# Top-k attention and a mixture of experts on one core: the first head pair in two halves of 128 tokens, and four places for fetched first parts

## Chip, cores, metric

One NeuronCore of a Trainium2 chip runs the whole program. The metric is the device time of one execution in microseconds (us). Engines: TensorE (PE; its weight loads PEld), VectorE (DVE), ScalarE (ACT), GpSimd (POOL) and SyncE (SP), which issues nearly all DMA transfers.

## What is computed

Four batches of eight heads with 576 tokens and head size 64: scores, the 32 largest of each row kept, softmax over them, times the values. The result, 2304 tokens of 512, goes through eight experts (512 to 1024, relu, back to 512), weighted per token by a gate that is normalised eight times over rows and columns.

```python
scores = scale * np.matmul(q, k.transpose(0, 1, 3, 2))
kth = np.partition(scores, -top_k, axis=-1)[..., -top_k:-top_k + 1]
scores = np.where(scores >= kth, scores, -1000000000.0)
attn = np.exp(scores - np.max(scores, axis=-1, keepdims=True))
attn = attn / (np.sum(attn, axis=-1, keepdims=True) + 1e-09)
x = np.matmul(attn, v)                # per head, then (2304, 512)
for e in range(E):
    h = np.maximum(x @ w1[e], 0.0)
    out += P[:, e:e + 1] * (h @ w2[e])   # P: normalised gate
```

## The kernel before, in words

**Attention.** Heads are taken in pairs (`attend_heads`), tokens in blocks of 256. Per head pair and block, `weight_tiles` takes two tiles of 128 tokens (t = 0, 1). For each tile and each of the two heads TensorE makes the scores (L122, L123), ScalarE copies them out of PSUM (`s`, L134), and VectorE finds the 32 largest in four rounds of the eight largest (L144) with three replacements between (L147), seven top-k operations per unit. ScalarE then weighs (L150, L151), GpSimd scales (L203), TensorE transposes (L274) and ScalarE stores the transposed weights in `at` (L291). After both tiles `weigh_values` multiplies with the values (L281), and ScalarE copies the result into the token tile `xt` (L304). `board` splits it into a high and a low part (`xh` on ScalarE by L83, `xl` on VectorE by L89).

**Experts.** `xh` and `xl` hold two seats of 256 tokens each: columns 0 to 255 and 256 to 511. A block sits in a seat for eight turns (`visit`), one expert per turn. Block 0 boards at turn 0, block 1 at turn 4, so in turns 0 to 3 (experts 0 to 3, `ALONE`) block 0 is alone and the second seat's columns stand idle. In those lone turns and the four after them (`LATER`, experts 4 to 7), part of the first layer of block 0 is made earlier, in plain fp32 from `xt`: `first_quarter` (L524, head pair 0 only, experts 4 to 7) and `first_half` (L537, head pairs 0 and 1, experts 0 to 3). Each result is copied out of PSUM (`y`, L512) and written to DRAM (L514). `second_half` fetches it again into one buffer `yp` (L546), multiplies the rest of the head pairs (L488) and adds the fetched part on VectorE (L552). `store_hidden` writes the hidden values (`hh` L556, `hl` L557), and L601 is the second layer.

**Order.** The program is written with priorities: attention high, the first parts low. A scheduler places the instructions of each engine in a fixed order; on the chip each engine, and SP's queue, works through its own order and waits at the head for what is not ready. Weights come into three buffers `wr`; `split_weights` converts them (`wh` on ScalarE L83, `wl` on GpSimd L86). Six such conversions for lone turn 0 are issued inside `first_half`. The places that the first parts take:

```python
for s in range(4):                                   # first_quarter, per expert
    ps = ps1.tile([128, 2, 256], F32, name="p1")     # ps1: two PSUM buffers
    for fo in range(2):
        nc.tensor.matmul(ps[:, fo, :], wr[:, s, fo * 128:(fo + 1) * 128], x[:, 0, :], start=True, stop=True)
    part(e, s, ps)                                   # ScalarE copy, then a write of 256 KB
```

Of the kernel before, what the change touches and what calls it, by code (L numbers as in the profile page):

```python
# [7 lines left out]
F32 = mybir.dt.float32  # L8
F32R = mybir.dt.float32r
U16 = mybir.dt.uint16  # L10
AF = mybir.ActivationFunctionType
# [4 lines left out]
DM, E, F = 512, 8, 1024  # L16
# [30 lines left out]
ALONE, LATER = range(0, 4), range(4, 8)  # L47
WR, WB, XR, NS, RAW, YB = 3, 6, 3, 3, 3, 4
# [3 lines left out]
def kernel(  # L52
# [11 lines left out]
    nc = tc.nc  # L64
    BIG = 1000000
# [181 lines left out]
        if not phases:  # L247
            attend_rest(hp, load_q("qm", 1024, 256, 1), ks, vr, xm)

    def weight_tiles(qs, ks, put, on_pool=False, crossed=None, plain=None):  # L250
        for t in range(2):
            Et = ap_.tile([128, 2, S], F32, name="Et", bufs=2)
            st = ap_.tile([128, 2, 2], F32, name="st", bufs=3)
            units = []
            for i in range(2):
                o = i * 256 + t * 128
                qc = qs[:, o:o + 128]
                if plain is not None and t == 0:
                    sp = plain_scores(plain[0][va if i == 0 else vb, o:o + 128], plain[1 + i][va if i == 0 else vb, :])
                else:  # L260
                    sp = scores([((a, 0, 288), [(qc, ks[i], slice(a * 288, a * 288 + 288))]) for a in range(2)])
                units.append((copy_scores(sp[:, :, 0:288]), Et[:, i, :], st[:, 0, i:i + 1]))
            topk(units, crossed is not None)
            normalise(Et, st, 2, on_pool)
            cs = slice(t * 128, (t + 1) * 128)
            if crossed is not None:
                cross(Et, crossed[:, :, cs])
                continue
            Ef = Et.rearrange("p a b -> p (a b)")
            for g in range(3):  # L270
                ps = pst.tile([128, 4, 128], F32, name="pt")
                for r in range(3):
                    j = g * 3 + r
                    nc.tensor.transpose(ps[:, r, :], Ef[:, j * 128:j * 128 + 128], idt)  # L274
                put(slice(g * 3, g * 3 + 3), cs, ps[:, 0:3, :])

    def weigh_values(av, vr, at, n, order):
        for j in order:
            for i, r in enumerate((va, vb)):
                o, block = (256 * i + 64 * j, 5 * i + j) if j < 4 else (512 + 64 * i, 4)  # L280
                weighed = nc.tensor.matmul(av[r, 0:n], vr[:, o:o + 64], at[:, block, 0:n], start=(j == order[0]), stop=(j == order[-1]))  # L281
        with tc.issue_after(weighed.ins):
            while ungated:
                gate_logits(*ungated.pop(0))

    def attend_phase(b, hp, qs, qm, ks, vr, xt, xm, plain=None):
        nq = 256 if xm is None else 320
        at = ap_.tile([128, 9, 320], F32, name="at", bufs=1)

        def put(blocks, cs, src):  # L290
            nc.scalar.activation(at[:, blocks, cs], src, AF.Copy)  # L291

        crossed = at if len(X) > 4 else None
        weight_tiles(qs, ks, put, b == 0 or crossed is not None, crossed, plain)
        if xm is not None:
            def put_rest(rows, blocks, src):
                nc.scalar.activation(at[rows, blocks, 256:320], src, AF.Copy)
            rest_weights(qm, ks, put_rest, None if crossed is None else at[:, :, 256:320])
        order = TAIL_FIRST if len(X) > 2 else range(5)

        def weigh():
            av = pst.tile([128, 512], F32, name="pt")
            weigh_values(av, vr, at, nq, order)
            nc.scalar.activation(xt[:, hp, :], av[:, 0:256], AF.Copy)  # L304
            if xm is not None:
                nc.scalar.activation(xm[:, hp, :], av[:, 256:320], AF.Copy)

        if turning:
            turning.append(weigh)
        else:  # L310
            weigh()
# [188 lines left out]


    PART = {}

    def half_weights(e, s2, half):
        wr = wp.tile([128, 2, 2, 256], F32, name="wr", bufs=WR)
# [4 lines left out]
    def part(e, s, ps):  # L510
# [2 lines left out]
        PART[e, s] = dram.tile([128, 512], F32, name=f"p{e}_{s}")  # L513
        nc.sync.dma_start(PART[e, s], y)  # L514

    def first_quarter(x):
        for e in LATER:
            wr = wp.tile([128, 4, 256], F32, name="wr", bufs=WR)
            for s in range(4):
                nc.sync.dma_start(wr[:, s], w1[e, s, :, 0, :])  # L520
            for s in range(4):
                ps = ps1.tile([128, 2, 256], F32, name="p1")
                for fo in range(2):
                    nc.tensor.matmul(ps[:, fo, :], wr[:, s, fo * 128:(fo + 1) * 128], x[:, 0, :],  # L524
                                     start=True, stop=True)
                part(e, s, ps)
# [15 lines left out]
        return got  # L542

    def second_half(e, s, seat, wh, wl, k0):
        y = ap_.tile([128, 512], F32, name="yp", bufs=1)
        nc.sync.dma_start(y, PART[e, s])  # L546
        y = y.rearrange("p (a b) -> p a b", a=2)
        ps = ps1.tile([128, 2, 256], F32, name="p1")
        products(ps, 0, seat, 256, wh, wl, k0)
        ft = slice(2 * s, 2 * s + 2)  # L550
# [330 lines left out]
```

## Time and profile before

| | |
|---|---|
| median of 3 runs | 1831.21 us (1831.04 to 1831.55) |
| profiled execution, its own time | 1833.39 us |
| its span | 1831.6 us |
| TensorE, weight loads | 1785.6 us busy (97%), 1480.7 (81%) |
| VectorE, ScalarE, GpSimd | 1207.9 us (66%), 1187.6 (65%), 1068.3 (58%) |
| moved by DMA | 270.77 MB, mean 148 GB/s |

Busy shares are means over stages with different limits, so an engine can be full in one stretch and half idle over the span. Of the waits a row names what came last by the profile. An engine that idles without being waited for costs nothing. A matmul with fp32 operands stands in the trace as two records of the same shape.

### The profile page before, as it was taken

The page shows a single profiled execution, that of the slowest core. Times are in us where ns is not written, and L with a number is a line of the kernel's source. Part 1 is how long each engine was busy: PE and PEld are TensorE (multiplying, and loading weights), DVE is VectorE, ACT ScalarE, POOL GpSimd, SP SyncE. Part 2 cuts the span into 40 slices and gives each one's busy share as a digit, 9 for nine tenths or more (in the row PEclk, how much of TensorE's full clock was granted, in tenths as well). Part 3 has the DMA queues.
Part 4 walks back from the last instruction along what each step waited for, and adds up shares of the span by engine and source line. Part 5 has one row for each costly group of instructions (what it writes and reads, how often), then busy time and mean ns, then how long its engine had stood idle before and what let it go on. Part 6 is the DMA issues. An engine that isn't in the chain of part 4 may idle for free.

```text
span 1831.6 us, 26304 instructions
## 1 busy us (share of the span) xinstructions
PE 1785.6 (97%) x9385; PEld 1480.7 (81%) x9385; DVE 1207.9 (66%) x2232; ACT 1187.6 (65%) x1785; POOL 1068.3 (58%) x842
## 2 busy tenths in 40 slices
PE   4989999999999999999999999999999999999998
PEld 3777888888888878777787889888888888888887
DVE  8999998988888878878787141255555555533333
ACT  5888899999999888988897645533333333333331
POOL 4367856656766585556564688955544554554441
PEclk9999999999999999999999999999999999999999
DMA  4885877765767575656655356423333333211111
GB/s 136 264 260 174 255 198 178 207 191 160 199 174 179 143 223 170 168 152 164 172 152 142 90 174 217 161 98 109 114 117 104 104 107 114 90 58 63 53 35 46
DMA packets 227203, 270.77 MB, mean 148 GB/s; under 512 B 142464, under 2 KB 146688, under 8 KB 227072
## 3 DMA queue, kind: packets, MB, share of 16 engines
q1 hardware_dynamic: 226928, 268.83, 49.8%
q8 instruction: 73, 1.20, 0.3%
q14 instruction: 58, 0.48, 0.1%
q10 hardware_dynamic: 144, 0.26, 0.0%
HBM read 202.19 MB, written 34.60 MB: 129 GB/s over the span
## 4 chain that ended last, share of the span: by engine, by line
PE 83%; ACT 4%; POOL 4%; DVE 3%; DMA 3%; issue 3%; SPq 0%; ACTq 0%; POOLq 0%
PE p L601 20%; PE p L775 19%; PE p L488 18%; PE p L713 10%; PE pc L713 5%; PE pt L281 4%; DMA wr<-in_w_dram 2%; PE pb L713 2%; POOL wl L86 2%; PE sp L122 2%; PE sp L123 2%; DVE m L144 1%; DVE w L147 1%; PE p L524 1%; ACT wh L83 1%
## 5 line engine op out<-in xcount | busy, mean ns | idle before, releaser
L86 POOL TENSOR_TENSOR wl<-wr,wh 128x1024 fp32r<-128x1024 f32 x288 | 694.0, 2422 | 456.2 <-ACT wh L83 445.7
L83 ACT ACTIVATE wh<-wr 128x1024 fp32r<-128x1024 f32 x288 | 304.1, 1061 | 284.4 <-PE p L713 191.2
L144 DVE MAX8 m<-w 128x8 f32<-128x576 f32 x432 | 320.6, 753 | 5.8
L488 PE MATMUL p<-xh,wh 128*128 128x256 f32 (+1 forms) x832 | 274.7, 330 | 2.8 <-DVE hl L557 1.9
L488 PE MATMUL p<-xl,wh 128*128 128x256 f32 (+1 forms) x832 | 273.7, 329 | 0.1
L488 PE MATMUL p<-xh,wl 128*128 128x256 f32 (+1 forms) x832 | 273.0, 328 | 0.0
L601 PE MATMUL p<-wh,hh 128*128 128x512 f32 x640 | 250.2, 396 | 4.3 <-ACT hh L556 2.8
L601 PE MATMUL p<-wl,hh 128*128 128x512 f32 x640 | 249.6, 392 | 0.0
L601 PE MATMUL p<-wh,hl 128*128 128x512 f32 x640 | 241.3, 392 | 0.0
L147 DVE MATCH_REPLACE8 w<-m,w 128x576 f32<-128x576 f32 x288 | 213.7, 743 | 0.0
L775 PE MATMUL p<-wh,h2h 128*128 128x512 f32 x512 | 199.1, 389 | 0.6 <-DVE acc L618 0.6
L775 PE MATMUL p<-wl,h2h 128*128 128x512 f32 x512 | 199.2, 389 | 0.0
L775 PE MATMUL p<-wh,h2l 128*128 128x512 f32 x512 | 196.3, 389 | 0.0
L618 DVE SCALAR_TENSOR_TENSOR acc<-p,P,acc 128x512 f32<-128x512 f32 x120 | 89.5, 750 | 160.4 <-PE p L775 160.4
L557 DVE SCALAR_TENSOR_TENSOR hl<-p,hh 128x512 fp32r<-128x512 f32 x160 | 109.0, 682 | 106.5 <-ACT hh L556 105.5
L488 PEld LDWEIGHTS p<-xh,wh 128*128 128x128 f32 x832 | 157.6, 189 | 20.8 <-issue 2.1
L488 PEld LDWEIGHTS p<-xl,wh 128*128 128x128 f32 x832 | 157.7, 189 | 15.7 <-issue 0.9
L488 PEld LDWEIGHTS p<-xh,wl 128*128 128x128 f32 x832 | 157.6, 189 | 14.2 <-issue 0.5
L144 DVE MAX8 m<-s 128x8 f32<-128x576 f32 x144 | 108.4, 753 | 85.3 <-ACT s L134 84.8
L601 PEld LDWEIGHTS p<-wh,hh 128*128 128x128 f32 x640 | 120.1, 188 | 31.7 <-ACT hh L556 5.3
L601 PEld LDWEIGHTS p<-wl,hh 128*128 128x128 f32 x640 | 120.6, 188 | 23.4 <-issue 0.4
L601 PEld LDWEIGHTS p<-wh,hl 128*128 128x128 f32 x640 | 119.9, 188 | 23.6 <-DVE hl L557 0.2
(171 smaller groups left out, 3550.4 us busy)
## 6 DMA issues: line engine op xcount, KB each, us to landing
wr<-in_w_dram SPq DMA_DIRECT2D x248, 512.0 KB, 3.5
y<-y SPq DMA_DIRECT2D x160, 256.0 KB, 2.8
raw<-in_k_dram SPq DMA_DIRECT2D x48, 288.0 KB, 3.7
p<-y SPq DMA_DIRECT2D x32, 256.0 KB, 4.0
wr<-in_w_dram SPq DMA_DIRECT2D x32, 256.0 KB, 4.3
yp<-p SPq DMA_DIRECT2D x32, 256.0 KB, 3.3
raw<-in_q_dram SPq DMA_DIRECT2D x31, 256.0 KB, 3.5
values<-in_v_dram SPq DMA_DIRECT2D x24, 256.0 KB, 3.6
```

Source lines behind the costliest of these rows:

```text
L83: nc.scalar.activation(dst, src, AF.Copy)
L86: nc.gpsimd.tensor_tensor(dst, src, hi.bitcast(F32), op=OP.subtract)
L122: nc.tensor.matmul(o, qc, kh[:, cs], start=(i == 0), stop=False)
L144: nc.vector.max(m8[:, u, r, :], ws[u] if r else units[u][0])
L147: nc.vector.match_replace(ws[u], m8[:, u, r, :], ws[u] if r else units[u][0], LOWEST)
L281: weighed = nc.tensor.matmul(av[r, 0:n], vr[:, o:o + 64], at[:, block, 0:n], start=(j == order[0]), stop=(j == order[-1]))
L488: nc.tensor.matmul(ps[:, fo, :], a[:, kk, fs], x[:, k0 + kk, cs], start=(i == 0), stop=(i == 3 * nk - 1))
L557: nc.vector.scalar_tensor_tensor(seat.hl[:, ft, cs], src, 0.0, seat.hh[:, ft, cs].bitcast(F32), op0=OP.max, op1=OP.subtract)
L601: nc.tensor.matmul(ps, a[:, ft, ts], m[:, ft % 2, :], start=(i == 0), stop=(i == 3 * NFT - 1))
L618: return nc.vector.scalar_tensor_tensor(ACC[t], y, g, ACC[t], op0=OP.mult, op1=OP.add)
L713: nc.tensor.matmul(ps, w[:, kk, :], x[:, kk, :], start=(fresh and i == 0), stop=(i == 5), skip_group_check=True)
L775: nc.tensor.matmul(ps, a[:, ft, ts], m[:, ft, :], start=(i == 0), stop=(i == 11))
```

## The change

Two things. First, for head pair 0 of the very first block (`plain` is set), the values are multiplied after each tile of 128 tokens (`then`), and after the first tile `first_eighths` loads the quarter weights of the last three experts (`QT = 3`: 5, 6, 7) and makes their first parts for these 128 tokens; `first_quarter` later makes the other 128 tokens from the same weights, and expert 4 as before. Each half result is written as 128 rows with two pieces of 128 columns, two writes of 128 KB per `y`. Second, in `second_half` the experts 0 to 3 fetch their first part into the columns 256 to 511 of `xh` (s = 0, 1) and `xl` (s = 2, 3), four places, where one buffer `yp` was; experts 4 to 7 keep `yp`.

```diff
-    def weight_tiles(qs, ks, put, on_pool=False, crossed=None, plain=None):
+    def weight_tiles(qs, ks, put, on_pool=False, crossed=None, plain=None, then=None):
         for t in range(2):
...
                 put(slice(g * 3, g * 3 + 3), cs, ps[:, 0:3, :])
+            if then is not None:
+                then(t)
-    def weigh_values(av, vr, at, n, order):
+    def weigh_values(av, vr, at, n, order, c0=0):
...
-                weighed = nc.tensor.matmul(av[r, 0:n], vr[:, o:o + 64], at[:, block, 0:n], start=(j == order[0]), stop=(j == order[-1]))
+                weighed = nc.tensor.matmul(av[r, 0:n], vr[:, o:o + 64], at[:, block, c0:c0 + n], start=(j == order[0]), stop=(j == order[-1]))
...
-        weight_tiles(qs, ks, put, b == 0 or crossed is not None, crossed, plain)
+        if plain is not None:
+            def then(t):
+                av = pst.tile([128, 512], F32, name="pt")
+                weigh_values(av, vr, at, 128, range(5), t * 128)
+                nc.scalar.activation(xt[:, hp, t * 128:t * 128 + 128], av[:, 0:128], AF.Copy)
+                if t == 0:
+                    with tc.high_priority(offset=-BIG):
+                        first_eighths(xt)
+
+            weight_tiles(qs, ks, put, True, None, plain, then)
+            return
+        weight_tiles(qs, ks, put, b == 0 or crossed is not None, crossed)
...
+    QT = 3
+    SPLIT = []
+
+    def first_eighths(x):
+        for e in range(E - QT, E):
+            wr = wp.tile([128, 4, 256], F32, name="wr", bufs=WR)
+            for s in range(4):
+                nc.sync.dma_start(wr[:, s], w1[e, s, :, 0, :])
+            SPLIT.append((e, wr))
+            eighths(e, wr, x, 0)
+
+    def eighths(e, wr, x, t):
+        for s2 in range(2):
+            ps = ps1.tile([128, 2, 2, 128], F32, name="p1")
+            for r in range(2):
+                for fo in range(2):
+                    nc.tensor.matmul(ps[:, r, fo, :], wr[:, 2 * s2 + r, fo * 128:(fo + 1) * 128], x[:, 0, t * 128:t * 128 + 128],
+                                     start=True, stop=True)
+            y = op_.tile([128, 512], F32, name="y", bufs=YB)
+            nc.scalar.activation(y, ps.rearrange("p r a b -> p (r a b)"), AF.Copy)
+            for r in range(2):
...
+                nc.sync.dma_start(PART[e, 2 * s2 + r].rearrange("p (a b) -> p a b", a=2)[:, :, t * 128:t * 128 + 128],
+                                  y[:, r * 256:r * 256 + 256].rearrange("p (a b) -> p a b", a=2))
+
     def first_quarter(x):
-        for e in LATER:
+        for e, wr in SPLIT:
+            eighths(e, wr, x, 1)
+        for e in list(LATER)[:len(LATER) - QT]:
...
     def second_half(e, s, seat, wh, wl, k0):
-        y = ap_.tile([128, 512], F32, name="yp", bufs=1)
-        nc.sync.dma_start(y, PART[e, s])
-        y = y.rearrange("p (a b) -> p a b", a=2)
+        if e in ALONE:
+            y = (xh, xl)[s // 2][:, s % 2 * 2:s % 2 * 2 + 2, 256:512].bitcast(F32)
+        else:
+            y = ap_.tile([128, 2, 256], F32, name="yp", bufs=1)
+        nc.sync.dma_start(y, PART[e, s].rearrange("p (a b) -> p a b", a=2))
```

**ScalarE, around the second tile of head pair 0 (some 33 to 43 us of the trace).** `kh` and `qs` are conversions for the next head pair, `at` the transposed weights, `s` the scores, `y` copies of first parts. Before:

```order
L151 ACTIVATE Et,st<-Et,eb 128x576 x2
L134 ACTIVATE s<-sp 128x576
L83 ACTIVATE kh<-raw 128x576
L83 ACTIVATE qs<-raw 128x512
L291 ACTIVATE at<-pt 128x3x128
L150 ACTIVATE Et<-s,m_420 128x576
L291 ACTIVATE at<-pt 128x3x128
L134 ACTIVATE s<-sp 128x576
```

Now, from the same L151 on:

```order
L300 ACTIVATE xt<-pt 128x128
L151 ACTIVATE Et,st<-Et,eb 128x576 x2
L134 ACTIVATE s<-sp 128x576
L548 ACTIVATE y<-p_196 128x512
L548 ACTIVATE y<-p_207 128x512
L83 ACTIVATE kh<-raw 128x576
L83 ACTIVATE qs<-raw 128x512
L548 ACTIVATE y<-p_223 128x512
L150 ACTIVATE Et<-s,m_468 128x576
L548 ACTIVATE y<-p_234 128x512
L293 ACTIVATE at<-pt 128x3x128 x2
L134 ACTIVATE s<-sp 128x576
```

Four copies of first parts came between the two copies of scores, and the first half of `xt` stands ahead of L151; two more `y` copies follow.

**SP's queue, at the first two experts of `first_half`.** `p` are the written first parts (expert's part, number), `wr` weights, `raw` keys of a later head pair. Before:

```order
L514 DMA p_0_540<-y 128x512
L507 DMA wr<-in_w_dram 128x512
L230 DMA raw<-in_k_dram 128x576
L546 DMA yp<-p_0_540 128x512
L507 DMA wr<-in_w_dram 128x512
L514 DMA p_1_549<-y 128x512
L514 DMA p_2_561<-y 128x512
L507 DMA wr<-in_w_dram 128x512 x2
```

Now:

```order
L528 DMA p_0_588<-y 128x512
L521 DMA wr<-in_w_dram 128x512 x2
L528 DMA p_1_597<-y 128x512
L590 DMA xh<-p_0_588 128x2x256
L230 DMA raw<-in_k_dram 128x576
L590 DMA xh<-p_1_597 128x2x256
L528 DMA p_2_609<-y 128x512
L521 DMA wr<-in_w_dram 128x512 x2
L528 DMA p_3_618<-y 128x512
L590 DMA xl<-p_2_609 128x2x256
L528 DMA p_0_630<-y 128x512
L521 DMA wr<-in_w_dram 128x512
```

All four first parts of lone turn 0 are fetched here, one or two issues behind the write that each reads (the fourth two rows further on); before, one of the four stood here and the other three stood behind the adds of the lone turn.

**TensorE, where head pair 3 ends and lone turn 0 begins.** L537 (now L578) are `first_half`, L281 (now L283) the values products, L488 (now L501) products of lone turn 0. Before:

```order
L537 MATMUL p_694<-xt,wr 128x256 x4
L281 MATMUL pt<-at,values 64x256 x10
L537 MATMUL p_706<-xt,wr 128x256 x4
```

Now, the last of `first_half` and what follows it:

```order
L578 MATMUL p_763<-xt,wr 128x256 x4
L122 MATMUL sp<-kh,qs 128x288
L123 MATMUL sp<-kl,qs 128x288
L122 MATMUL sp<-kh,qs 128x288
L123 MATMUL sp<-kl,qs 128x288
L501 MATMUL p_2891<-xh,wh 128x256
L501 MATMUL p_2891<-xl,wh 128x256
L501 MATMUL p_2891<-xh,wl 128x256
L274 MATMUL pt<-idt,Et 128x128 x3
L283 MATMUL pt<-at,values 64x256 x3
```

Two groups of `first_half` stood behind head pair 3's values products; now all of `first_half`, and the products of lone turn 0 that need head pair 2 alone, stand ahead of them.

## Rows read from the trace of the kernel before

**Rows 1.** The page, busy time, share of the span, instructions.
```profile
PE 1785.6 (97%) x9385; PEld 1480.7 (81%) x9385; DVE 1207.9 (66%) x2232; ACT 1187.6 (65%) x1785; POOL 1068.3 (58%) x842
```
**Rows 2.** Stretches: length; busy PE, PEld, DVE, ACT, POOL; granted clock, DMA share, GB/s.
```profile
34.00:40.00 6.00, 4.91 (x20) 3.31 (x21) 6.00 (x14) 4.31 (x10) 4.31 (x5) 1.00 0.11 22
40.00:46.00 6.00, 4.03 (x25) 2.85 (x25) 6.00 (x15) 3.51 (x8) 1.23 (x4) 0.94 0.40 121
46.00:54.00 8.00, 7.59 (x35) 6.14 (x33) 7.82 (x17) 6.14 (x12) 1.79 (x3) 0.83 0.39 139
54.00:62.00 8.00, 7.06 (x37) 6.02 (x38) 7.96 (x18) 8.00 (x19) 4.93 (x7) 1.00 0.97 300
62.00:70.00 8.00, 8.00 (x49) 5.73 (x48) 7.47 (x18) 6.96 (x16) 1.66 (x3) 1.00 0.99 331
```
**Rows 3.** Timeline of TensorE, 45 to 120 us: start, length, instruction.
```profile
45.05 3.37 PE L524 MATMUL p<-xt,wr 128*128 128x256 f32 x8
...
49.11 1.89 PE L524 MATMUL p<-xt,wr 128*128 128x256 f32 x8
50.84 0.49 PE L274 MATMUL pt<-idt,Et 128*128 128x128 f32 x3
...
111.43 2.38 PE L281 MATMUL pt<-at,values 128*64 128x256 f32 x20
113.74 1.99 PE L537 MATMUL p<-xt,wr 128*128 128x256 f32 x8
...
116.43 1.89 PE L537 MATMUL p<-xt,wr 128*128 128x256 f32 x8
...
119.27 0.38 PE L488 MATMUL p<-xl,wh 128*128 128x256 f32 x1
```
**Rows 4.** Timeline of VectorE, 40 to 120 us; in brackets the idle time before.
```profile
40.09 0.74 DVE L144 MAX8 m<-s 128x8 f32<-128x576 f32 x1
...
89.26 0.76 DVE L144 MAX8 m<-s 128x8 f32<-128x576 f32 x1 [3.01 <-ACT s L134]
...
106.96 0.76 DVE L144 MAX8 m<-s 128x8 f32<-128x576 f32 x1 [0.92 <-ACT s L134]
...
117.24 1.97 DVE L89 TENSOR_TENSOR xl<-xt,xh 128x256 fp32r<-128x256 f32 x1 [1.66 <-ACT xh L83]
```
**Rows 5.** Stretch at lone turn 0, columns as in rows 2.
```profile
120.00:140.00 20.00, 17.25 (x139) 14.10 (x138) 19.97 (x42) 16.39 (x34) 14.13 (x14) 1.00 0.75 239
```
**Rows 6.** Timeline of ScalarE, 35 to 116 us.
```profile
35.83 0.68 ACT L83 ACTIVATE kh<-raw 128x576 fp32r<-128x576 f32 x1 [1.18 <-PE sp L122]
...
38.62 0.65 ACT L134 ACTIVATE s<-sp 128x576 f32<-128x576 f32 x1
...
46.75 0.60 ACT L512 ACTIVATE y<-p 128x512 f32<-128x512 f32 x1 [1.68 <-PE p L524]
...
85.73 1.06 ACT L83 ACTIVATE wh<-wr 128x1024 fp32r<-128x1024 f32 x1 [3.65 <-DMA wr<-in_w_dram]
...
115.43 1.06 ACT L83 ACTIVATE wh<-wr 128x1024 fp32r<-128x1024 f32 x1 [2.91 <-DMA wr<-in_w_dram]
```
**Rows 7.** DMA issues from 45 to 120 us: totals; count, size, median us to landing.
```profile
DMA packets 10855, 19.78 MB, mean 264 GB/s; under 512 B 1632, under 2 KB 2144, under 8 KB 10848
...
p<-y SPq DMA_DIRECT2D x31, 256.0 KB, 4.0
```
**Rows 8.** Groups of VectorE, 120 to 262 us: count, busy us, mean ns, idle before.
```profile
L552 DVE TENSOR_TENSOR p<-p,yp 128x512 f32<-128x512 f32 x20 | 13.8, 688 | 1.8 <-PE p L488 1.5 <-DMA yp<-p 0.2
```
**Rows 9.** Timeline of SP's issues, 71 to 80 us.
```profile
71.43 1.95 SPq L514 DMA_DIRECT2D p<-y  x2
...
77.78 0.33 SPq L546 DMA_DIRECT2D yp<-p  x1
...
79.62 1.06 SPq L507 DMA_DIRECT2D wr<-in_w_dram  x2
```
**Rows 10.** What SP's queue waited for, 27 to 130 us: total us, times, longest.
```profile
SPq L546 <- DMA p<-y: 2.2, 1, 2.2
```

More of the change, by code (lines that the diff above doesn't have):

```diff
@@ L514, in part @@
         nc.sync.dma_start(PART[e, s], y)
+    SPLIT = []
[16 more added lines that the diff above has]
+            for r in range(2):
+                if (e, 2 * s2 + r) not in PART:
+                    PART[e, 2 * s2 + r] = dram.tile([128, 512], F32, name=f"p{e}_{2 * s2 + r}")
+                nc.sync.dma_start(PART[e, 2 * s2 + r].rearrange("p (a b) -> p a b", a=2)[:, :, t * 128:t * 128 + 128],
+                                  y[:, r * 256:r * 256 + 256].rearrange("p (a b) -> p a b", a=2))
     def first_quarter(x):
-        for e in LATER:
+        for e, wr in SPLIT:
+            eighths(e, wr, x, 1)
+        for e in list(LATER)[:len(LATER) - QT]:
             wr = wp.tile([128, 4, 256], F32, name="wr", bufs=WR)
```

## Prediction

> **What bounds the kernel now.** I read the page's busy times first: TensorE is busy for 1785.6 us, 97% of the span [rows 1], so its 46 us of idle time are all that any reordering can win. Next the stretches of the opening [rows 2]. From 34 to 46 us TensorE works 4.91 and 4.03 of 6 us each, VectorE all 12, and the DMA engines are loaded at 0.11 and 0.40, from 46 to 54 at 0.39. From 54 to 70 us they are full (0.97 and 0.99). So up to about 45 us TensorE lacks work that is ready, and after that the weights press on the DMA engines.
>
> Then TensorE's own rows [rows 3]. The first parts begin at 45.05 us, the last group of `first_half` (L537) at 116.43 us, and at 119.27 us stands the first product of lone turn 0 (L488) that reads the low part of head pair 3. VectorE delivers that low part with the `xl` that starts at 117.24 us and takes 1.97 [rows 4]. TensorE's spare work therefore runs out just as block 0 is attended. Behind that point VectorE is the full engine: 19.97 of 20 us from 120 to 140, where TensorE has 17.25 [rows 5].
>
> So the question is not how early TensorE gets work, but how long VectorE stands still. From 51 to 120 us it has three waits: 3.01, 0.92 and 1.66 us, 5.6 us in all, each put down to ScalarE [rows 4]. ScalarE itself stood at 85.73 us for 3.65 us and at 115.43 us for 2.91 us, both times with a weight conversion at the head of its queue and the weights not landed [rows 6]. DMA, through ScalarE's queue, stops VectorE.
>
> **Part 1: opening per 128 tokens, on TensorE.** Of the 32 matmuls of `first_quarter` (two records each in the trace) 24 become 48 of half the columns, and half of these go ahead of 45.05 us. Eight records of 256 columns take 50.84 - 49.11 = 1.73 us [rows 3], 0.216 each, so I estimate 0.108 for 128 columns. 48 records make 5.2 us moved into idle time. I count 0 of it. In the order, head pair 3's values products stand behind all but two groups of `first_half` before and behind all of it after, and lone turn 0 cannot end before VectorE has finished head pair 3; what TensorE gains before, it waits there. The cover is VectorE's chain of top-k rounds; if that were not the bound, it would be -5.2. The values products of head pair 0 become 40 records where 20 took 113.74 - 111.43 = 2.31 us, 0.116 each [rows 3]: between nothing and 20 x 0.058 = 1.2 us more, half of it in idle time and the rest ahead of the same VectorE chain. 0 again.
>
> **Part 2: the same on ScalarE.** Six copies of partial results at 0.60 us [rows 6] and a second `xt` copy of some 0.3 us go into the stretch from 33 to 46 us, in all 3.9 us. ScalarE had 1.69 + 2.49 = 4.2 us free between 34 and 46 [rows 2]. They fit in sum, but the order puts four of them ahead of the copy of scores that stood at 38.62 us. 2.4 us of copies meet an idle gap of 1.18 us there [rows 6], and VectorE takes the result at 40.09 us [rows 4], 0.8 us after it was written. The two `y` copies behind add 1.2 us in front of the next scores, where ScalarE had more idle time. So VectorE is late by 0 if every gap is used, by 3.9 if none is. I take +1.0, nearer to the first, because the free time exceeds the added time.
>
> **Part 3: on the DMA engines.** The early halves are 12 writes of 128 KB, 1.57 MB. At 264 GB/s, the mean from 45 to 120 us [rows 7], that is 6.0 us of transfer which leaves the full stretch and goes where the load was 0.11 to 0.40 [rows 2]. Against it, three more fetches of 256 KB (0.79 MB, 3.0 us) now stand before the first conversions, as the four places fill early. Weights then land about 3.0 us earlier. That removes 3.0 of ScalarE's 3.65 us and all of its 2.91, and of VectorE's waits 3.01 x 3.0/3.65 = 2.5 and 1.66, together 4.1. Of this I give back 0.7 for SP: it has 12 more issues of 0.3 to 0.5 us [rows 9], and fetches that stand directly behind the write they read. I take -3.4; the bounds are -5.6 (all three waits gone) and 0 (the DMA engines stay as full as they are).
>
> **Part 4: four places.** In the lone turns, VectorE's adds waited 0.2 us for the fetched first part and 1.5 for products [rows 8]. Four places can remove the first, -0.2. Other waits there are VectorE's own work. What is late next: block 1 boards only when the last adds have read the second seat's columns. The order then issues four pairs of ScalarE and VectorE copies that before were spread over the lone turns; the first `hl` of the second seat has the same 272 top-k rounds before it in both programs, so this costs 0.
>
> **The sum:** 0 + 1.0 - 3.4 - 0.2 = -2.6 us. The profiled execution took 1833.39 us (span 1831.6 and 1.8 around it), so it would become 1830.8. It stood 2.2 us above the median of 1831.21, so against the runs the forecast is **1828.6 us**. A measurement of this kernel can tell about 0.2% from no change, 3.7 us: below 1827.5 is faster, above 1834.9 slower.
>
> **Rival 1: TensorE's lead is kept.** TensorE is 97% busy, which speaks for it; VectorE's 19.97 of 20 us [rows 5] speak against it. Then the 5.2 us count. So does the clock: the first eight records after TensorE's idle time took 3.37 us against 1.89 for the next eight [rows 3], and with work before them those 1.5 us go too. -6.7 us, 1824.5. The Trainium skill (TensorE: Matmul & The Clock Gate, Part 1) has the array at 1.2 GHz after idling and at 2.4 GHz once it has been busy; by that rule the trace agrees, since 3.37 is nearly twice 1.89. By the page the earlier work would pay twice, by the row on VectorE neither payment reaches the end.
>
> **Rival 2: slower, because fetches hold SP's queue.** In the program before, one fetch of a first part stands among the opening's weights: written from 71.43 us on, fetched at 77.78, weights issued at 79.62 [rows 9]. It held SP for 2.2 us [rows 10]. Now four such fetches stand between the writes and the weights of the first conversions (order of SP). Three more holds of 2.2 are 6.6 us, less the 3.0 us by which the DMA engines are relieved: the weights land 3.6 us later, ScalarE waits that much longer, and VectorE with it. With +1.0 and -0.2 that is +4.4, **1835.6 us**. It decides from the point at which the first conversion on ScalarE waits longer than the 3.65 us of before. For it: the holds are certain, since a write took 4.0 us to land in this stretch [rows 7]. Against it: the weights also wait for a free buffer, so holds and buffer waits overlap. The Trainium skill (DMA: Bandwidth & Descriptors, Anatomy of one DMA) speaks against the change here: a transfer has a fixed cost of about 2.0 us, mostly the confirmation of the write, and a wait on it is spent on the issuing sequencer. By its figure three holds would be 6.0 us and the rival 1835.0 (an estimate from the page); by the row it is 1835.6.
>
> **Rival 3: it cancels.** The DMA engines remain full because the early fetches replace the writes that left, and part 3 is 0: 1.0 - 0.2 = +0.8, 1832.0. For it: 0.97 and 0.99 of load [rows 2]. Against it: ScalarE's longest wait, at 85.73 us, comes right behind the full stretch, so what leaves that stretch reaches it.
>
> **How the numbers follow.** Forecast 0.42, lead kept 0.24, cancelled 0.20, slower 0.14. The forecast's own spread (part 3 between -4.5 and -1.5) runs from 1827 to 1831; with some of it below 1827.5, faster has 0.24 + 0.13 = 0.37. Of the slower rival 0.10 lies above 1834.9. The rest, 0.53, is no change that can be told. The range from 1824.0 to 1834.0 takes in rival 1, the forecast and rival 3 and leaves out most of rival 2 and the far end of part 3, together less than 0.2.
>
> **What would show it.** Right: TensorE has work at 33 to 36 us; ScalarE's waits for weights between 75 and 120 us fall from 6.6 us to about 1; VectorE's waits in the opening shrink by 3 to 4 us; TensorE waits several us more before lone turn 0's products than it does now. Wrong: if TensorE's idle time before the first lone turn falls by 5 us and stays away, rival 1 holds; if the first conversion on ScalarE waits over 3.65 us, rival 2; if VectorE stands still more than 1 us between 38 and 47 us, part 2 was too small.

## The result, and the profile after

The change makes the kernel **slower by 0.5%**: 1841.11 us, median of 6 runs (1835.26 to 1842.69), where the kernel before takes 1831.17 (1830.30 to 1831.55). The ratio is 1.0051, 95% interval 1.0037 to 1.0064, some 9 us. The forecast was 1828.6 us, with a range up to 1834.0. The profiled execution took 1842.69 us.

The page of the kernel after, span and busy times (those of before are [rows 1]):

```profile
span 1840.9 us, 26469 instructions
...
PE 1786.2 (97%) x9453; PEld 1482.4 (81%) x9453; DVE 1203.9 (65%) x2232; ACT 1188.9 (65%) x1786; POOL 1069.1 (58%) x842
```

TensorE is as busy as before, 1786.2 us against 1785.6 [rows 1]. So in this execution the longer span, 1840.9 against 1831.6 us, is idle time of TensorE: 54.7 against 46.0 us. (A second profile of the same program, from the run after_again, splits otherwise: 1790.7 us busy and 52.0 idle.) Where the idle time lies is read from three stretches (length; busy time and records of PE, PEld, DVE, ACT, POOL; granted clock, DMA share, GB/s). Before:

```profile
62.00:140.00 78.00, 71.17 (x435) 57.59 (x434) 71.74 (x150) 63.66 (x127) 44.00 (x45) 0.98 0.83 270
140.00:320.00 180.00, 176.56 (x1135) 150.73 (x1134) 169.97 (x341) 159.16 (x251) 127.66 (x109) 0.98 0.71 201
320.00:700.00 380.00, 377.95 (x2222) 316.29 (x2221) 319.38 (x628) 350.51 (x519) 242.26 (x208) 1.00 0.66 182
```

After:

```profile
62.00:140.00 78.00, 64.88 (x393) 50.93 (x394) 67.33 (x143) 59.89 (x118) 41.52 (x44) 0.98 0.81 261
140.00:320.00 180.00, 174.76 (x1127) 149.42 (x1126) 168.72 (x340) 159.51 (x253) 128.26 (x108) 0.98 0.68 198
320.00:700.00 380.00, 374.73 (x2186) 313.36 (x2186) 304.58 (x604) 342.93 (x498) 238.86 (x202) 1.00 0.66 180
```

Length less busy PE is TensorE's idle time: 6.8, 3.4 and 2.1 us before, 13.1, 5.2 and 5.3 us after. In the first 62 us it fell by 1.5 us, as the early first parts intend, and behind 700 us it is 1.1 us less. The new idle time stands behind the place that was edited, and 5 us of it from 140 to 700 us (4.7 in the second profile), where the change does nothing but fetch into other places.

Who is waited for in the opening, 62 to 140 us (total us, times, longest)? TensorE's wait for weights before, then its largest waits after:

```profile
PE p L537 <- DMA wr<-in_w_dram: 0.3, 1, 0.3
```

```profile
PE p L578 <- DMA wr<-in_w_dram: 4.4, 3, 2.0
PE p L578 <- ACT y L526: 4.3, 4, 1.8
```

ScalarE's timeline after, 59 to 86 us, shows a wait of a new kind:

```profile
59.37 0.60 ACT L526 ACTIVATE y<-p 128x512 f32<-128x512 f32 x1 [0.90 <-DMA p<-y]
61.12 0.60 ACT L526 ACTIVATE y<-p 128x512 f32<-128x512 f32 x1 [1.16 <-DMA p<-y]
65.58 0.60 ACT L526 ACTIVATE y<-p 128x512 f32<-128x512 f32 x1 [2.55 <-DMA p<-y]
85.00 1.06 ACT L83 ACTIVATE wh<-wr 128x1024 fp32r<-128x1024 f32 x1 [2.49 <-DMA wr<-in_w_dram]
```

The copies of first parts wait until a write has landed and a `y` buffer is free; the program has four of them. The first conversion waits 2.49 us where it waited 3.65 [rows 6]. VectorE's waits from 51 to 120 us have grown from 6.3 to 10.6 us. Before, then after:

```profile
DVE m L144 <- ACT s L134: 4.1, 3, 3.0
DVE xl L89 <- ACT xh L83: 2.2, 2, 1.7
```

```profile
DVE m L144 <- ACT s L134: 7.0, 6, 2.3
DVE st L200 <- POOL st L199: 2.6, 1, 2.6
DVE xl L89 <- ACT xh L83: 1.0, 1, 1.0
```

Head pair 3's low part, which lone turn 0 needs, starts 8.3 us later than the 117.24 us of before [rows 4]:

```profile
125.54 0.41 DVE L89 TENSOR_TENSOR xl<-xt,xh 128x256 fp32r<-128x256 f32 x1
```

So three suspects stood at once: the `y` buffers, the fetches and weights on SP's queue, and stretches of the program that the edit does not touch.

### The profile page after: what moved, and what is told of

It reads as the page before. It is cut to its first block, busy times and chain, and to the rows that moved or that the text cites. A ratio compares the mean times of both kernels' runs of the same rounds, so it can differ in the third digit from the quotient of the medians.

```text
span 1840.9 us, 26469 instructions
## 1 busy us (share of the span) xinstructions
PE 1786.2 (97%) x9453; PEld 1482.4 (81%) x9453; DVE 1203.9 (65%) x2232; ACT 1188.9 (65%) x1786; POOL 1069.1 (58%) x842
## 4 chain that ended last, share of the span: by engine, by line
PE 73%; ACT 9%; DVE 7%; DMA 5%; issue 3%; POOL 2%; SPq 0%; ACTq 0%; POOLq 0%
PE p L818 19%; PE p L644 15%; PE p L501 15%; PE p L756 9%; PE pc L756 5%; DVE m L144 3%; DVE w L147 3%; PE pt L283 3%; PE pb L756 2%; DMA turned<-halves 2%; ACT at L171 2%; PE sp L122 1%; DMA wr<-in_w_dram 1%; PE sp L123 1%; ACT Et L151 1%
## 5 line engine op out<-in xcount | busy, mean ns | idle before, releaser
L501 PE MATMUL p<-xh,wh 128*128 128x256 f32 (+1 forms) x832 | 275.4, 331 | 6.5 <-DVE hl L600 4.3
L501 PE MATMUL p<-xl,wh 128*128 128x256 f32 (+1 forms) x832 | 273.5, 329 | 0.0
L501 PE MATMUL p<-xh,wl 128*128 128x256 f32 (+1 forms) x832 | 272.9, 329 | 0.0
L501 PEld LDWEIGHTS p<-xh,wh 128*128 128x128 f32 x832 | 157.9, 190 | 26.5 <-DVE hl L600 7.5
L501 PEld LDWEIGHTS p<-xl,wh 128*128 128x128 f32 x832 | 158.0, 190 | 15.1 <-issue 0.5
L501 PEld LDWEIGHTS p<-xh,wl 128*128 128x128 f32 x832 | 157.9, 190 | 14.6 <-issue 0.8
```

The costliest lines, as they stand in the source:

```text
L501: nc.tensor.matmul(ps[:, fo, :], a[:, kk, fs], x[:, k0 + kk, cs], start=(i == 0), stop=(i == 3 * nk - 1))
```

## The experiments

All ratios are to the kernel before, timed beside each run; us are ratio less one, times its median.

| run | ratio, 95% interval | us |
|---|---|---|
| the change | 1.0051 (1.0037 to 1.0064) | +9.3 |
| split_alone | 1.0082 (1.0069 to 1.0095) | +15.0 |
| places_alone | 1.0164 (1.0145 to 1.0182) | +30.0 |
| staged | 1.0066 (1.0050 to 1.0081) | +12.1 |
| whole | 1.0035 (1.0023 to 1.0047) | +6.4 |
| split_held | 0.9988 (0.9979 to 0.9997) | -2.2 |
| places_held | 0.9995 (0.9986 to 1.0004) | -0.9 |
| both_held | 0.9986 (0.9977 to 0.9995) | -2.6 |
| before_reordered | 1.0080 (1.0066 to 1.0094) | +14.7 |
| opening_held | 1.0046 (1.0034 to 1.0059) | +8.4 |
| rest_held | 1.0015 (1.0006 to 1.0023) | +2.7 |
| late_held | 1.0048 (1.0036 to 1.0060) | +8.8 |
| thin | 1.0060 (1.0047 to 1.0073) | +11.0 |
| held_to_320 | 1.0033 (1.0020 to 1.0045) | +6.0 |
| held_from_320 | 1.0022 (1.0012 to 1.0033) | +4.0 |
| hh_first | 1.0056 (1.0043 to 1.0068) | +10.3 |
| after_again | 1.0056 (1.0043 to 1.0068) | +10.3 |

### Each half of the change by itself

The split alone:

```diff
     def second_half(e, s, seat, wh, wl, k0):
-        if e in ALONE:
-            y = (xh, xl)[s // 2][:, s % 2 * 2:s % 2 * 2 + 2, 256:512].bitcast(F32)
-        else:
-            y = ap_.tile([128, 2, 256], F32, name="yp", bufs=1)
+        y = ap_.tile([128, 2, 256], F32, name="yp", bufs=1)
```

> The opening per 128 tokens as in the change, but every fetched first part goes back to the one buffer. Theory A (the split writes of 128 KB keep the four y buffers occupied, ScalarE's y copies wait for them, and VectorE behind ScalarE): nearly the whole loss is here, 1838 to 1841 us, with the same waits of ScalarE for p<-y between 59 and 66 us (4.6 us in sum). Theory B (four fetches, each directly behind the write that it reads, hold SP's queue and the weights come late): about 1831 us, and TensorE's waits for wr at 92 and 106 us (3.8 us) are gone. Theory C (the lone turns themselves: fetches placed earlier change the order there): about 1831 us as well, and no stall of TensorE near 185 us.

The places alone (the kernel before, with this part of the change):

```diff
-        y = ap_.tile([128, 512], F32, name="yp", bufs=1)
-        nc.sync.dma_start(y, PART[e, s])
-        y = y.rearrange("p (a b) -> p a b", a=2)
+        if e in ALONE:
+            y = (xh, xl)[s // 2][:, s % 2 * 2:s % 2 * 2 + 2, 256:512].bitcast(F32)
+        else:
+            y = ap_.tile([128, 2, 256], F32, name="yp", bufs=1)
+        nc.sync.dma_start(y, PART[e, s].rearrange("p (a b) -> p a b", a=2))
```

> The program before with the four places alone. Theory A: 1830 to 1832 us, no change. Theory B: 1836 to 1841 us, with TensorE waiting for wr several us between 85 and 110 us. Theory C: 1834 to 1841 us with a stall of TensorE of 3 us or more in a lone turn, 140 to 320 us, and the opening as it was before. If the parts add up, the difference of this one and that of the split alone sum to +9.9 us.

None of the three theories had this: +15.0 and +30.0 us, and +9.3 for both together. Parts that each cost more than the whole can hardly be costs of the parts. What the three have in common stands in the order of the instructions. A scheduler lays out the whole program again after each edit: in the places alone, ScalarE's 1641 instructions follow the old order for the first 113 and part from it there, though that edit removes no instruction and adds none. In the change itself they part after the first 24 of 1642.

### The `y` buffers and the form of the writes

In these two, the queues of TensorE and VectorE are those of the change, instruction for instruction. The diffs are cut.

```diff
+            i = len(STAGED)
+            STAGED.append((e, s2, t))
+            if i % 2 == 0:
+                y = (xh, xl)[i // 2 % 4 // 2][:, i // 2 % 2 * 2:i // 2 % 2 * 2 + 2, 256:512]
...
-            y = op_.tile([128, 512], F32, name="y", bufs=YB)
+            else:
+                y = op_.tile([128, 512], F32, name="y", bufs=YB)
```

> The whole change, but every second y copy of the split experts goes into one of four places in the second seat's token columns (rounded to the products' format), so that eight y buffers serve the opening where four do now. Theory A: ScalarE's waits for p<-y (4.6 us between 59 and 66 us) fall below 1 us, and the time to 1832 to 1835 us. Theory B: 1839 to 1842 us, as the change. Theory C: 1839 to 1842 us.

```diff
-            for r in range(2):
...
+            nc.sync.dma_start(WHOLE[e, s2][:, t, :], y)
```

> The whole change, but a y buffer of the split experts is written by one transfer of 256 KB in rows of 2 KB (12 writes where there are 24 with rows of 512 B), and read back in two pieces when block 0 boards the last experts' turns. Theory A in its form that the number and the small rows of the writes hold the buffers: ScalarE's waits for p<-y between 59 and 66 us halve or more, 1833 to 1837 us. If it is only that writes take 4 us to land whatever their form, the waits stay and so does the time, 1839 to 1842 us. Theories B and C: 1839 to 1842 us.

What ScalarE's `y` copies waited for writes, 40 to 70 us: 4.6 us in the change, then staged and whole.

```profile
ACT y L526 <- DMA p<-y: 3.1, 1, 3.1
```

```profile
ACT y L526 <- DMA p<-y: 1.2, 2, 0.7
```

The wait shrinks by a third and by three quarters. The time does not follow in the first (+12.1 us); in the second it is some 3 us less (+6.4, its interval still overlapping that of the change). The buffers are held as theory A says, but they are a small part of the loss at most: TensorE still waits 5.0 and 3.5 us for weights in the opening.

### The order held

Now the same programs with the order of before. A table gives each engine's instructions in the order wanted, and each is tied to the one ahead of it by an edge that sets order alone (new instructions, and the boarding copies that the places force back, stand elsewhere):

```diff
+    for engine, seq in table.items():
+        ins = [i for i in nc.cur_bb.bb.instructions if ...]
+        for a, b in zip(seq, seq[1:]):
+            tc.add_manual_dep(ins[b], ins[a].name, DependencyInfo(NoSync, DATA), reason="held")
```

> The opening per 128 tokens alone, but every engine's queue is held to the order of the program before by a table (edges that set the order and wait for nothing); only the new instructions stand where the scheduler put them in the split alone. Theory D (the scheduler, which orders the whole program anew after each edit, made a worse order, and the edit itself costs nothing): 1825 to 1832 us, TensorE's idle time from 62 to 140 us at 8 us or less. Theory E (the edit's own costs, writes and copies in the opening, are the loss, whatever the order): 1838 to 1848 us, as the split alone in the scheduler's order (1848.3). Between 1833 and 1837 us both have a share.

> The four places alone, all queues held to the order of the program before, but for three pairs of block 1's boarding copies that have to move behind the last fetch of a lone turn. Theory D: 1830 to 1834 us where the scheduler's own order of the same program took 1862.5. Theory E: above 1850 us.

> The whole change (split and places), queues held to the order of the program before, with the boarding copies moved as in the places held. Theory D: within 1.5 us of the split held, so 1825 to 1833 us. Theory E: 1838 to 1843 us, as the change.

> The program before, unchanged in its work, but its queues held to the order that the scheduler made for the split alone (the first quarters undivided, at the places of the second eighths). Theory D: slower than before by most of what the split alone lost, 1840 to 1850 us. Theory E: 1829 to 1834 us, since no write or copy is added.

All four came out for theory D. In before's order the change is **faster** than before, 2.6 us (interval 0.9 to 4.2); the places, 30 us slower in their own order, make no difference that can be told. And the kernel before, with not one instruction more or less, loses 14.7 us in the order of the split alone, which had lost 15.0. The order is the loss, and it is shown from both sides. The edges themselves are not the gain: late_held and hh_first below tie the queues in the same way to the change's own order, with a few instructions moved, and are at +8.8 and +10.3 us. One thing the held order leaves out: the fetches into the places stand where the fetches of before stood (SP issues them at 74.60, 119.52, 124.63 and 131.48 us; before at 77.78 [rows 9], 124.28, 129.63 and 134.60), so an early fetch is not part of what is timed here.

The held change's stretches:

```profile
62.00:140.00 78.00, 70.99 (x436) 57.83 (x436) 74.61 (x156) 63.33 (x126) 46.29 (x45) 1.00 0.80 262
140.00:320.00 180.00, 176.07 (x1153) 151.16 (x1152) 167.12 (x341) 162.78 (x255) 125.88 (x108) 0.99 0.70 204
320.00:700.00 380.00, 376.66 (x2199) 314.10 (x2199) 318.40 (x627) 347.80 (x514) 241.35 (x207) 1.00 0.67 182
```

TensorE idles 7.0, 3.9 and 3.3 us there, close to before; its wait for weights in the opening is 0.2 us, where the change's own order has 4.4, with the same writes, copies and fetches in the program:

```profile
PE p L578 <- DMA wr<-in_w_dram: 0.2, 1, 0.2
```

### Where the order loses

The cut at 140 us, in words (the first run has all behind the opening in the change's own order, the second the opening alone):

```diff
-ORDER = before's order, the new instructions inserted
+ORDER = before's order up to about 140 us, the change's order behind it
```

> The whole change; up to about 140 us (179 instructions of ScalarE, 470 of TensorE) every queue in the order of the program before, behind that in the order that the scheduler gave the change. If the loss of the change (+9.9 us) arises in the opening's order, this one is at -3 to +2 us against before. If it arises in the lone turns behind it, +7 to +12 us. From the idle times of TensorE (+6.5 us from 62 to 140 us, +5 us behind) I expect about +2.5 us (half of the order's 12.4 us kept).

> The mirror image: the opening in the order that the scheduler gave the change, and from about 140 us on the order of the program before. If the opening's order is the cause, +7 to +12 us against before; if the order behind it, -3 to +2 us. I expect about +5 us; the two should add up to the change's +9.9 and the held change's -2.5 us.

The expectation had half and half. It is +8.4 us with the opening alone in the old order and +2.7 with all that follows it in the old order: by both runs the larger part of the loss lies behind 140 us, though the two parts do not simply add up (the opening's order is worth 0.9 us from one end and 5.3 from the other). The second cut, at 320 us:

> The whole change, every queue in the order of the program before up to about 320 us (405 instructions of ScalarE), behind that in the change's own order. With the cut at 140 us it was +8.0 us against before. If the lone turns from 140 to 320 us hold the loss: -2 to +2 us. If it lies behind 320 us: +6 to +9 us. From TensorE's idle times in the trace with the cut at 140 us (140 to 200 us 6.5 us where the held change has 3.1; 320 to 700 us 6.6 where it has 3.3) I expect about half, +3 to +5 us.

> The mirror image: the change's own order up to about 320 us, the order of the program before behind it. With the cut at 140 us it was +2.0 us. If the lone turns hold the loss: +7 to +10 us; if it lies behind 320 us: +1 to +3 us; I expect +4 to +7 us.

From no order held (the change, +9.3) by the opening held (+8.4) and up to 320 us held (+6.0) to all of it held (-2.6), the steps are 0.9, 2.4 and 8.6 us. From the other end, 6.3 us are saved behind 320 us (+10.3, measured with this run, to +4.0), 1.3 from 140 to 320, 5.3 in the opening. Each step is uncertain by some 3 us, by the intervals. From the first end the largest lies clearly **behind 320 us**, where the split adds no instruction and the places are no longer in use; from the other end it is 6.3 against 5.3 us, which cannot be told apart. So no one stretch is shown to hold the loss.

The stretch behind 320 us, held up to there:

```profile
320.00:700.00 380.00, 373.42 (x2152) 311.03 (x2152) 302.54 (x599) 339.38 (x498) 237.12 (x202) 0.99 0.66 178
```

and what TensorE waits for in it (total, times, longest):

```profile
PE p L501 <- DVE hl L600: 3.4, 4, 2.0
PE sp L122 <- ACT s L134: 3.0, 2, 2.0
```

6.6 us of idle time against 3.3 with the order held throughout, nearly all of it in six waits of up to 2.0 us for VectorE's low parts and ScalarE's scores.

### Three repairs inside the change's own order

SP's queue alone, the four fetches behind the last weights of the first halves; TensorE's, ScalarE's and VectorE's queues untouched (in words):

```diff
-p weights xh<-p(0) ... xh<-p(1) ... weights xl<-p(2) ... weights xl<-p(3) ... weights
+p weights ... weights ... weights xh<-p(0) xh<-p(1) xl<-p(2) xl<-p(3)
```

> The change in its own order on every engine; only on SP's queue the four fetches of lone turn 0 move from between the writes that they read (75 to 86 us) to behind the last weights of the first halves (105 us). Theory B (fetches behind their own writes hold SP's queue and the weights behind them): TensorE's waits for wr between 62 and 140 us fall from 4.4 us to under 1.5, and the time by 3 to 5 us, to +5 to +7 us against before. If the order of the weights among themselves and the buffers that free them are the cause: the waits stay above 3 us and the time at +8 to +11 us.

TensorE's waits, 62 to 140 us:

```profile
PE p L578 <- ACT y L526: 4.4, 3, 3.0
PE p L578 <- DMA wr<-in_w_dram: 4.0, 3, 1.7
```

What SP waited for at these fetches, 27 to 130 us, in the change and then here:

```profile
SPq L590 <- DMA p<-y: 5.7, 4, 2.3
```

```profile
SPq L590 <- DMA p<-y: 1.6, 1, 1.6
```

The fetches did hold SP, but with most of the holds gone TensorE's wait for weights stays (4.0 for 4.4 us) and so does the time, +8.8: theory B falls. Next, the bytes. Of the early parts only 16 of 128 rows are written, the others are left out (cut):

```diff
-                    PART[e, 2 * s2 + r] = dram.tile([128, 512], F32, name=f"p{e}_{2 * s2 + r}")
+                    PART[e, 2 * s2 + r] = dram.tile([16, 512], F32, name=f"p{e}_{2 * s2 + r}")
...
-                                  y[:, r * 256:r * 256 + 256].rearrange("p (a b) -> p a b", a=2))
+                                  y[0:16, r * 256:r * 256 + 256].rearrange("p (a b) -> p a b", a=2))
```

> The change in its own order, but of the first eighths only 16 of 128 partitions are written to memory (the fetches read these 16 rows eight times over; the other rows are left out). 24 writes of 128 KB become 24 of 16 KB, 2.75 MB less, 10 us of the DMA engines at 264 GB/s. If the full DMA engines of the opening set TensorE's waits: 4 to 8 us faster than the change, +2 to +6 us against before. If the order sets them: within 2 us of the change, +8 to +11 us.

2.75 MB less, and +11.0 us. So the bytes of the new writes are not the loss. But nearly all of them leave the stretch in front, 33 to 62 us, where the DMA engines were busy for 0.65 (the change, then here):

```profile
33.00:62.00 29.00, 24.00 (x177) 20.72 (x178) 28.73 (x62) 24.60 (x52) 12.11 (x17) 1.00 0.65 185
```

```profile
33.00:62.00 29.00, 23.72 (x177) 20.77 (x178) 29.00 (x63) 25.50 (x54) 12.10 (x17) 1.00 0.35 101
```

From 62 to 140 us the load hardly moves, 260 for 261 GB/s, so this run is no test of that stretch. TensorE's largest wait there:

```profile
PE p L578 <- DMA wr<-in_w_dram: 3.6, 2, 2.0
```

It has 3.6 us where it had 4.4. What speaks on the load of the full stretch is the held change above: with 262 GB/s and a share of 0.80 from 62 to 140 us, TensorE waits 0.2 us for weights. So the load alone does not set these waits, the order does; whether by the time at which each weight is asked for or by the time at which its buffer comes free is not shown. Last, a single place. In the change, TensorE stood 3.97 us for a `hh` that began at 184.16 us; VectorE's add in front of it had ended at 181.40, but on ScalarE's queue a weight conversion, a copy of transposed weights, a weighing and the conversions of keys and queries stood ahead:

```profile
180.72 0.68 DVE L595 TENSOR_TENSOR p<-p,xh 128x512 f32<-128x512 f32 x1
```

```profile
184.16 0.61 ACT L599 ACTIVATE hh<-p 128x512 fp32r<-128x512 f32 x1
```

```profile
184.82 0.80 PE L644 MATMUL p<-wh,hh 128*128 128x512 f32 x1 [3.97 <-ACT hh L599]
```

```diff
-wh  at  Et  kh  qs  hh  wh  s  qm  hh
+wh  hh  at  Et  kh  qs  hh  wh  s  qm
```

> The change in its own order, but for ScalarE's queue at 181 to 187 us: two hh copies move ahead of the copies of scores, keys and weights that stand in front of them (four and three instructions). TensorE's stall of 3.97 us at 184.82 us falls to about 1.5 us, since VectorE's add was done at 181.3. If such places are the loss, the time falls by 1.5 to 3 us against the change; if TensorE's idle time only moves to the next wait, by less than 1 us.

> The change itself, as it is, on the same chip as the three others: 8 to 11 us slower than before, as first measured (+9.9).

The change again (its second profile, with a shorter wait at the same place), and then with the two copies moved, TensorE's timeline there:

```profile
182.77 0.50 PE L644 MATMUL p<-wh,hh 128*128 128x512 f32 x1 [2.06 <-ACT hh L599]
```

```profile
183.26 1.16 PE L274 MATMUL pt<-idt,Et 128*128 128x128 f32 x6 [1.52 <-POOL Et L203]
```

The wait for `hh` is gone, TensorE stands 1.52 us for GpSimd's `Et` half a microsecond later, and from 140 to 320 us it idles 3.1 us for 3.3. Both programs take +10.3 us. Here one place mended moved the wait to the next.

## Why the prediction was wrong

**The step that failed is the sum's missing term for the order.** The prediction priced each moved step where it stood and wrote of the rest "so this costs 0" (part 4, of what is late next, from the order of the copies that board block 1). It compared a few places of the order and took the rest of ScalarE's 1642 instructions as they were. They were not: the whole program had been laid out anew. In the old order the change is at -2.6 us; the new order is worth some +12 on top (-2.6 to +9.3), and the sum has nothing for it. By its own steps:

- **Part 1, TensorE's lead, 0.** For idle time it fits. The early matmuls start at 33.12 us:

```profile
33.12 2.05 PE L545 MATMUL p<-xt,wr 128*128 128x128 f32 x16 [1.11 <-ACT xt L300]
```

  In the held change TensorE idles 1.6 us less before 62 us, but over the whole 46.8 us, 46.0 before. So the lead is lost again, and the half of rival 1 that saves idle time is out. It is not lost where the forecast had it: the several us more of waiting before lone turn 0 did not come (7.0 us of idle time from 62 to 140 us, 6.8 before).
- **Part 2, ScalarE, +1.0.** Too much. In the held change VectorE stands 0.22 us in all from 38 to 47 us, in the change's own order not at all; the copies found their gaps.
- **Part 3, weights earlier by 3.0 us, -3.4 in all.** The first links are there in the held change, and not in the change's own order. Its conversions and VectorE's waits:

```profile
83.00 1.06 ACT L83 ACTIVATE wh<-wr 128x1024 fp32r<-128x1024 f32 x1 [2.56 <-DMA wr<-in_w_dram]
...
112.30 1.06 ACT L83 ACTIVATE wh<-wr 128x1024 fp32r<-128x1024 f32 x1 [2.64 <-DMA wr<-in_w_dram]
```

```profile
86.54 0.76 DVE L144 MAX8 m<-s 128x8 f32<-128x576 f32 x1 [0.86 <-ACT s L134]
...
104.09 0.76 DVE L144 MAX8 m<-s 128x8 f32<-128x576 f32 x1 [0.99 <-ACT s L134]
...
114.11 1.98 DVE L89 TENSOR_TENSOR xl<-xt,xh 128x256 fp32r<-128x256 f32 x1 [1.40 <-ACT xh L83]
```

  The weights land 2.7 us earlier (83.00 for 85.73) and 3.1 (112.30 for 115.43 [rows 6]), and head pair 3's low part starts 3.1 us earlier (114.11 for 117.24 [rows 4]). VectorE's waits of 51 to 120 us fall from 6.3 to 3.3 us (the prediction had counted 5.6, the three longest of five). One sign was wrong: ScalarE's waits for weights hardly shrink (6.8 to 6.4 us in sum), because ScalarE itself arrives earlier, 1.6 us at the first of these conversions and 2.9 at the last. In the change's own order they fall to 5.4 and VectorE's waits grow to 10.6 all the same.
- **Part 4, the places, -0.2.** Nothing that can be told (0.9995, interval 0.9986 to 1.0004), in an order that fetches no earlier than before.
- **Rival 2** named 1835.6 us, nearest to the result, for a reason that is not it. Its own point of decision, a first conversion that waits over 3.65 us, was not reached (2.49), and late_held, which takes most of the holds away, gives nothing back that can be told. The Trainium skill (DMA: Bandwidth & Descriptors, Anatomy of one DMA) has a wait on a semaphore spent on the issuing sequencer; the trace agrees, SP stood for 5.7 us in four such waits. (That section is on DMAs issued by GpSimd, those here are issued by SyncE, so its 2.0 us, used in the prediction, is a figure from a neighbouring path.) That the waits cost time does not follow: with 1.6 us of them left, the time is the same.
- **Rival 3** (+0.8 us) is neither the change (+9.3) nor the held change (-2.6, interval -4.2 to -0.9).

**That the held change comes out at the forecast's -2.6 us is luck.** Part 3 took 6.0 us of relief of the DMA engines and gave back 3.0 for three early fetches. In the held order these fetches are not early, so the relief alone should have brought the weights 6.0 us forward, and it brought 2.7 and 3.1. Nor is VectorE's lead seen to become time: its boarding copy (`xl`) that stood at 609.48 us before is at 606.39, 3.1 us ahead, the one at 861.14 is at 860.52, 0.6 ahead, and TensorE idles no less over the whole (46.8 for 46.0 us). What the traces show as gained is busy time of TensorE, 1783.9 us for 1785.6 [rows 1] (1782.5 in the split held, with 46.3 us idle). The page of the held change:

```profile
span 1830.7 us, 26457 instructions
...
PE 1783.9 (97%) x9453; PEld 1480.8 (81%) x9453; DVE 1204.9 (66%) x2232; ACT 1187.6 (65%) x1786; POOL 1068.1 (58%) x842
```

The mean granted clock points the same way, 0.9973 over the held change's eleven runs against 0.9964 over the 27 beside it: times the span some 1.5 of the 2.6 us (an estimate, and a loose one: the two means differ by less than twice their uncertainty). That is the clock half of rival 1, for which the forecast had nothing. How much of the rest goes by VectorE's waits stays open.

The rival that mattered was not among the three: that the edit comes with a new order of everything. Three new orders were timed with an edit that the held order shows to be worth -2.6 to 0 us (the change, the split, the places): +9.3, +15.0 and +30.0 us. An honest range would have reached some 30 us above the sum.

What stays open: why the new orders are worse. The scheduler makes them from a simulated timeline; that its durations are what is off is not shown here. Nor was it tried whether some order beats the held one, or whether before's own order was a lucky one among many. The held change, 1830.92 us where before took 1833.46 beside it (0.9986, 0.9977 to 0.9995), beats both kernels.

## What to carry to other kernels

Where a scheduler lays out the program, an edit and the order that comes with it are two changes: hold the queues to the old order by edges and time the edit alone before judging it. Before forecasting, count how far each queue still agrees with the old one; where it parts early, the range has to take in what a new order costs, here 0.5 to 1.6% against 0.14% for the edit. A single stall in a full program need not be the price: the one mended here handed its time to the next wait. And before an experiment is read as a test of a loaded stretch, look whether it lightened that stretch.

## What was not expected of the hardware

**In one order the clock took a third of the loss.** The places alone run the matmuls of before, 9385 records both, but TensorE is busy 1795.0 us where it was 1785.6 [rows 1], so 9.4 of the 26.2 us of longer span are busy time. The page, TensorE's timeline and a stretch:

```profile
PE 1795.0 (97%) x9385; PEld 1487.6 (80%) x9385; DVE 1204.7 (65%) x2232; ACT 1188.8 (64%) x1785; POOL 1068.3 (58%) x842
```

```profile
36.43 0.61 PE L122 MATMUL sp<-kh,qs 128*128 128x288 f32 x1 [4.35 <-ACT s L134]
36.83 0.45 PE L123 MATMUL sp<-kl,qs 128*128 128x288 f32 x1
...
47.13 0.29 PE L122 MATMUL sp<-kh,qs 128*128 128x288 f32 x1
```

```profile
33.00:62.00 29.00, 23.40 (x107) 17.26 (x108) 29.00 (x64) 22.95 (x47) 11.79 (x17) 0.82 0.50 160
```

Behind an idle time of 4.35 us a score of 288 columns takes 0.45 us, and 0.29 ten microseconds on; the granted clock over the stretch is 0.82, where the change, with its early first parts in that gap, has 1.00. The Trainium skill (TensorE: Matmul & The Clock Gate, Part 1) has two levels, 1.2 GHz after idling and 2.4 GHz when busy; the rows agree in direction. Over its five runs the places alone were granted 0.9902 of the clock on average, the kernel before 0.9958 over the eleven beside them; times the span that is some 10 of the 30 us (an estimate). It is not so in every order: the split alone has 0.9950, some 1.5 of its 15.0 us. And one profile's busy time is a weak witness: the change was profiled at 1786.2 and at 1790.7 us.

**The same load, with and without the waits.** From 62 to 140 us the change's own order moves 261 GB/s with the DMA engines busy for 0.81 of the time, and TensorE waits 4.4 us for weights; the held change moves 262 at 0.80, and TensorE waits 0.2 us; before, it was 270 at 0.83, and 0.3 us. DMA engines as busy as this did not by themselves make the weights late.
